# Moving the stops at which VectorE's small steps are emitted, from unit 10 on, in an attention and token-MLP kernel

## The chip, the cores and the metric

One core of one Trainium2 chip. The metric is the device time of one execution in microseconds. The change was timed in six runs of each kernel. The profiler takes one more execution of each kernel.

## The reference, cut to what matters

```python
x  = A_x                                   # 1 x 2048 x 1024, bf16
xn = layernorm(x)
out = x + A(xn, wq, wk, wv, wo, beta) + B(xn, w1, b1, w2, b2)
# A: 32 heads of 32, four segments of 512 tokens: in each a masked softmax attention and a read of a
#    memory that sums phi(k) v over the earlier segments, mixed by a gate; then the projection wo
# B: layernorm, then an MLP over the tokens (2048 -> 3584 -> 2048) with gelu
```

## The kernel before

The attention runs as 32 units, one for each segment and group of four heads. A unit computes logits, exponentials and the weighted sums (`weigh`) of its group, and between them fills TensorE (PE) with projection jobs of eight 512-column matmuls each: V, output projection (`wo`), Q, K. VectorE (DVE) empties PSUM banks and also runs small steps on SBUF data: `scales`, `phi_q`, `products`, the sum of the two products with the transpose of the result, and `phi_k` with a transpose. The steps wait in a list, `side`. While the program writes down a job's matmuls, it takes one step from that list at each of the job's stops, which are places among the eight matmuls. "Unit 11's steps" are those written down in unit 11.

```python
STOPS = ((1, 4, 7), (1, 4))                # jobs ended by ScalarE; jobs ended by VectorE
STOPS_FEW = ((1, 3, 5, 7), (1, 3, 5))

def dense(self, n, side=True):
    while n > 0 and self.jobs:
        at, b, reads, mm, end, on_dve = self.jobs[0]
        stops = self.stops[on_dve] if side else ()
        ...                                # b: the job's PSUM bank
        stop = min(at + n, 8)
        if self.side and side:
            stop = min([stop] + [x for x in stops if x > at])
        with fw.group(reads=reads(), writes=[self.R_bank[b]]):   # its last matmul increments a semaphore
            for i in range(at, stop):
                mm(b, i)
        ...
        if stop == 8:
            end(b)                         # empties the bank: ScalarE for V and Q, VectorE for wo and K
            self.jobs.popleft()
        elif self.side and stop in stops:
            self.side.popleft()()          # one small step
```

```python
# in proj_job, when a Q or K job is complete: load the weights two units ahead, then empty the bank
def finish(b):
    if u + 2 < N_UNIT:
        ring.ensure(u + 2)                 # a DMA issued by SyncE (SP)
    end(b)

# in attention(), unit u
total = 8 * len(self.jobs) - sum(j[0] for j in self.jobs) - self.left
...
self.stops = self.STOPS_FEW if total <= 26 and u >= 14 else self.STOPS
```

Each engine executes its instructions in the order in which they were written for it. Where one depends on another engine, the helper writes a wait for the semaphore of the last access to the tile concerned.

## Time and profile before

| | |
|---|---|
| time | 652.76 us median of 6 runs (652.47 to 652.96) |
| span in the profile | 651.1 us, granted PE clock 1.000 |
| PE busy | 645.8 us of it |
| DVE busy | 428.1 us |

PE is the bound, and only its gaps can be won. In the window of the change the two largest stand at the end of a run of DVE work. This is DVE's timeline for the steps of unit 11 and the first evictions of unit 12; the columns are start, duration, engine, source line, operation, tiles, shapes and count, and idle time before it in brackets:

```profile
480.00 1.65 DVE L1478 TENSOR_TENSOR prod<-ost,srec 128x1024 bf16<-128x1024 bf16 x1
481.68 0.74 DVE L1484 TENSOR_TENSOR o_s<-prod 128x512 bf16<-128x512 bf16 x1
482.34 0.28 DVE L1241 TENSOR_SCALAR mtmp<-etmp 128x512 bf16<-128x512 bf16 x1
482.65 0.69 DVE L1243 SCALAR_TENSOR_TENSOR mtmp<-kT,mtmp 128x512 bf16<-128x512 bf16 x1
483.26 0.68 DVE L1275 CAST kT<-ps_all 128x512 bf16<-128x512 f32 x1
483.87 1.04 DVE L1431 TENSOR_TENSOR ost<-ps_all,eps 128x396 bf16<-128x396 f32 x2
```

No line has idle time before it: DVE goes from products, sum and phi_k straight to the copy of K and the evictions of `ost`. PE, in unit 12 at 484.48 us, waits for the first of these evictions. The other wait stands at 503.74 us in unit 14, behind the steps of unit 13.

### The profile page before, as it was taken

Reading aid. Unit: us, or ns where it says so; the run is one execution under the profiler, and the core shown is the slowest. Engines: PE = TensorE matmul, PEld = TensorE weight load, DVE = VectorE, ACT = ScalarE, POOL = GpSimd, SP = SyncE. Lnnn points to the kernel's source line nnn. Section 1 sums busy time; section 2 is a strip of 40 time slices with the busy share of each in tenths; the row PEclk is TensorE's granted clock in tenths of the full one; section 3 lists DMA queues with packets and bytes.
Section 4 is the critical chain, followed back from the end, with each engine's and each line's share of the span. In section 5 each row is a group of like instructions: output and inputs, shape, how many; then the busy total and the mean of one; then the engine's idle time right before and its main releaser. Section 6 shows DMA issues by size and latency. Waiting matters only on the chain.

```text
span 651.1 us, 11170 instructions
## 1 busy us (share of the span) xinstructions
PE 645.8 (99%) x4611; PEld 303.2 (47%) x4611; DVE 428.1 (66%) x800; ACT 281.4 (43%) x305; POOL 153.9 (24%) x179
## 2 busy tenths in 40 slices
PE   8999999999999999999999999999999999999998
PEld 3444444444444444444444444444544444445544
DVE  6975675665556664744738325766787877777896
ACT  7543232232210000110101047778767778888770
POOL 2500000000011220220202203343334444554440
DMA  9804233242498967538262946988544456445325
GB/s 306 212 0 130 65 106 89 64 116 79 129 257 206 270 205 209 156 103 229 80 208 98 267 126 174 179 169 197 120 116 96 125 147 109 126 98 128 106 93 139
DMA packets 181963, 95.00 MB, mean 146 GB/s; under 512 B 100248, under 2 KB 167832, under 8 KB 181656
## 3 DMA queue, kind: packets, MB, share of 16 engines
q1 hardware_dynamic: 181768, 94.25, 56.3%
q8 instruction: 36, 0.59, 0.4%
q14 instruction: 15, 0.12, 0.1%
q10 hardware_dynamic: 144, 0.03, 0.0%
HBM read 69.23 MB, written 13.63 MB: 127 GB/s over the span
## 4 chain that ended last, share of the span: by engine, by line
PE 91%; DVE 5%; ACT 2%; DMA 2%; issue 1%; POOL 0%; DVEq 0%
PE ps_all L199 91%; ACT pT L1377 1%; DMA w2s<-in_B_w_dram 1%; DVE prod L1478 1%; DVE ln_st L587 1%; DVE sum L648 0%; DMA xin<-in_A_x_dram 0%; DVE mtmp L1243 0%; DVE h L627 0%; DVE mtmp L1241 0%; DVE fin L1320 0%; DVE ost L1431 0%; DVE kT L1275 0%; POOL ln_rs L611 0%; DVE part L689 0%
## 5 line engine op out<-in xcount | busy, mean ns | idle before, releaser
L1377 ACT ACTIVATE pT<-ps_all 128x2048 bf16<-128x2048 f32 x80 | 150.2, 1877 | 47.7 <-PE ps_all L199 47.2
L1381 POOL TENSOR_SCALAR_AFFINE_SELECT pT<-pT 128x512 bf16<-128x512 bf16 x128 | 105.3, 841 | 161.3 <-ACT pT L1377 161.3
L689 DVE TENSOR_TENSOR part<-ps_all,part 128x512 f32<-128x512 f32 x84 | 57.7, 690 | 109.1 <-PE ps_all L199 88.2
L1080 POOL TENSOR_TENSOR part<-part,stg 128x512 f32<-128x512 f32 x24 | 33.0, 1403 | 285.5 <-DVE part L689 285.5
L746 ACT ACTIVATE g<-part,b1c 128x512 f16<-128x512 f32 x36 | 26.0, 722 | 99.1 <-DVE part L689 99.1
L199 PE MATMUL ps_all<-wv,xnT 128*128 128x512 bf16 x256 | 68.6, 380 | 0.2
L199 PE MATMUL ps_all<-xnT,wq 128*128 128x512 bf16 (+1 forms) x256 | 66.4, 380 | 0.0
L199 PE MATMUL ps_all<-wo,oT 128*128 128x512 bf16 (+2 forms) x272 | 63.8, 367 | 0.1
L1431 DVE TENSOR_TENSOR ost<-ps_all,eps 128x396 bf16<-128x396 f32 (+1 forms) x72 | 37.1, 522 | 33.9 <-PE ps_all L199 33.3
L694 ACT ACTIVATE part<-ps_all 128x512 f32<-128x512 f32 x24 | 14.0, 596 | 101.6 <-PE ps_all L199 67.1
L199 PEld LDWEIGHTS ps_all<-vA,pT 128*128 128x128 bf16 x1280 | 45.7, 96 | 20.4 <-DVE ost L1431 1.7
L199 PE MATMUL ps_all<-g,w2s 128*128 128x512 f16 x224 | 51.0, 379 | 0.0
L199 PE MATMUL ps_all<-g,sum 128*128 128x512 f16 x224 | 51.0, 379 | 0.0
L199 PE MATMUL ps_all<-gT,sum 128*128 128x512 f16 x224 | 50.3, 379 | 0.2 <-DVE gT L663 0.2
L199 PE MATMUL ps_all<-vA,pT 128*128 128x33 bf16 x1280 | 48.5, 177 | 0.3 <-DVE ost L1431 0.3
L199 PE MATMUL ps_all<-h,sum 128*128 128x512 f16 x192 | 45.2, 379 | 0.0
L199 PE MATMUL ps_all<-h,w1s 128*128 128x512 f16 x192 | 44.9, 379 | 0.0
L199 PE MATMUL ps_all<-hT,sum 128*128 128x512 f16 x192 | 43.6, 379 | 0.0
L199 PEld LDWEIGHTS ps_all<-wo,oT 128*128 128x128 bf16 x272 | 23.8, 98 | 24.7 <-issue 3.7
L199 PEld LDWEIGHTS ps_all<-xnT,wq 128*128 128x128 bf16 x256 | 22.6, 97 | 25.4 <-issue 5.3
L199 PEld LDWEIGHTS ps_all<-gT,sum 128*128 128x128 f16 x224 | 21.8, 98 | 26.8 <-DVE gT L663 0.6
L199 PEld LDWEIGHTS ps_all<-g,w2s 128*128 128x128 bf16 x224 | 21.9, 98 | 26.4
(118 smaller groups left out, 867.7 us busy)
## 6 DMA issues: line engine op xcount, KB each, us to landing
w2s<-in_B_w_dram SPq DMA_DIRECT2D x8, 1792.0 KB, 9.7
w1s<-in_B_w_dram SPq DMA_DIRECT2D x12, 1024.0 KB, 5.6
wq<-in_A_wq_dram SPq DMA_DIRECT2D x32, 256.0 KB, 3.2
stg<-in_A_x_dram SPq DMA_DIRECT2D x16, 256.0 KB, 2.9
xs<-in_A_x_dram SPq DMA_DIRECT2D x16, 256.0 KB, 3.3
out_dram<-stg SPq DMA_DIRECT2D x16, 256.0 KB, 3.7
wk<-in_A_wk_dram SPq DMA_DIRECT2D x16, 256.0 KB, 3.6
fin<-out_dram SPq DMA_DIRECT2D x16, 256.0 KB, 3.3
```

The lines of the kernel that those rows point to most:

```text
L199: ins = self.nc.tensor.matmul(*args, **kwargs)
L587: fw.op("dve", lambda e: e.bn_stats(st[:, 6 * h:6 * h + 6], src[:, 512 * h:512 * h + 512]), reads=[self.R_xin[c]], writes=[R])
L689: self.fw.op("dve", lambda e: e.tensor_tensor(self.tmp[dst][:], self.bank(b), self.tmp[src][:], op=ALU.add), reads=[self.R_bank[b], self.R ...
L694: self.fw.op("act", lambda e: e.activation(self.tmp[dst][:], self.bank(b), ACT.Copy), reads=[self.R_bank[b]], writes=[self.R_tmp[dst]])
L746: self.fw.op("act", lambda e: e.activation(self.gB[f % 2][half][:, f // 2, :], src, ACT.Gelu_apprx_tanh, bias=self.b1c[:, f:f + 1], scale= ...
L1080: fw.op("pool", lambda e: e.tensor_tensor(self.tmp[t][:], self.tmp[t][:], self.stg[k][:, 512 * half:512 * half + 512], op=ALU.add), reads= ...
L1377: fw.op("act", lambda e: e.activation(dst, src, ACT.Exp, scale=SCALE), reads=self.R_bank[0:4], writes=[R[v % 2][kb] for v, kb, _ in blocks ...
L1381: fw.op("pool", lambda e: e.affine_select(d, d, pattern=[[0, 4], [1, P]], compare_op=ALU.is_ge, fill=0.0, base=0, channel_multiplier=-1), ...
L1431: fw.op("dve", lambda e: e.tensor_tensor(dst, src, eps, op=ALU.add), reads=[self.R_bank[b], self.R_eps], writes=[self.R_ost[o][part]])
L1478: fw.op("dve", lambda e: e.tensor_tensor(self.prod[:], ost[:, :, 0:D_HEAD], rec.unsqueeze(2).to_broadcast([P, 32, D_HEAD]), op=ALU.mult), ...
```

## The change

Its intent, read from its form, is to spread the small steps more evenly over the jobs. From unit 10 on they come at matmuls 1, 3, 5 and 7 instead of 1, 4 and 7, and in jobs that VectorE ends at 1 and 3 instead of 1 and 4, unless the first branch takes the unit.

```diff
     STOPS = ((1, 4, 7), (1, 4))
+    STOPS_MID = ((1, 3, 5, 7), (1, 3))
     STOPS_FEW = ((1, 3, 5, 7), (1, 3, 5))
...
-            self.stops = self.STOPS_FEW if total <= 26 and u >= 14 else self.STOPS
+            self.stops = self.STOPS_FEW if total <= 26 and u >= 14 else self.STOPS_MID if u >= 10 else self.STOPS
```

(Worked out from the job list no unit from 14 on has more than 24 matmuls left, so the first branch takes them all. Only units 10 to 13 get the new stops.)

## The prediction

> **What bounds the kernel now.** I read the page first: the busy times, then the chain of work that ended last.
>
> ```profile
> span 651.1 us, 11170 instructions
> ...
> PE 645.8 (99%) x4611; PEld 303.2 (47%) x4611; DVE 428.1 (66%) x800; ACT 281.4 (43%) x305; POOL 153.9 (24%) x179
> ...
> PE 91%; DVE 5%; ACT 2%; DMA 2%; issue 1%; POOL 0%; DVEq 0%
> ```
>
> TensorE (PE) is busy 645.8 of 651.1 us, and is 91% of the chain. A change that removes no matmul can only win back PE's gaps, 651.1 - 645.8 = 5.3 us, 0.8% of the span. A gain of over 2% (13 us) is out of reach.
>
> The diff names units 10 to 17 of the attention (32 units of one head group each). A unit's stops are chosen as "few" first where it has at most 26 matmuls and is number 14 or later. I worked each unit's count out from the job list: units 10 to 13 have four jobs (V, output projection, Q, K), 32 matmuls; units 14 to 17 have three, 24, and so keep the stops they have. The change reaches only units 10 to 13. In the timeline they run from the first output projection (465.6 us) to some 505 us. The table of stretches gives for that window:
>
> ```profile
> core 0: us, PE busy (x) PEld busy (x) DVE busy (x) ACT busy (x) POOL busy (x), PEclk, DMA share, GB/s
> 466.00:505.00 39.00, 38.55 (x393) 18.64 (x392) 32.32 (x64) 26.92 (x27) 13.64 (x16) 1.00 0.44 102
> ```
>
> PE's gaps are 39.00 - 38.55 = 0.45 us here: all that a perfect reordering of VectorE (DVE) in these units could win, 0.07%. The list of waits of that window says whose they are:
>
> ```profile
> PEld ps_all L199 <- DVE ost L1431: 1.3, 2, 0.7
> ...
> PE ps_all L199 <- DVE ost L1431: 0.3, 2, 0.2
> ```
>
> Twice PE waits for DVE to empty a bank (columns: total, times, longest). The chain shows why: DVE runs prod, o_s, mtmp, the copy of kT and then that eviction back to back. This is what the author presumably wants to ease.
>
> **What the Trainium skill says.** "Trainium Architecture — The Big Picture", section "Inside one NeuronCore": each engine has its own instruction stream, and they meet only through semaphores. So the place of a DVE step among the matmuls in the source means nothing in itself; only its order on DVE and its waits do. The trace agrees: DVE's o_s starts at 471.81 us, as soon as prod (470.55 + 1.22 us) is over, while PE is inside a run of V matmuls. "DMA: Bandwidth & Descriptors", section "Queues, rings and completion order": SP owns one queue row, whose descriptors each DMA engine takes in ring order. The trace shows the half of it that matters here, SP's issues one after another, each 0.4 to 2 us. "TensorE: Matmul & The Clock Gate", section "The cost: per-tile semaphore tail": about 26 ns for each increment that a packed matmul makes. No view of this trace isolates that.
>
> **The change part by part.** I compared the two built programs engine by engine, with each wait traced back to the instruction that releases it.
>
> PE: the same 4,611 matmuls in the same order with the same releasers. Ten semaphore increments go from one matmul to a neighbour (from the fourth to the third, from the seventh to the fifth, and so on): ten added, ten taken away, net 0. Were all ten pure cost at the page's 26 ns it would be an estimated 0.26 us, 0.04%.
>
> DVE, ACT, POOL: the same instructions, the same order, the same releasers. The reason: the steps (scales, phi, products, sum) read and write SBUF only, so none waits for a matmul; and in each of the four units the same steps fall between the same bank evictions. One more step is emitted inside Q's job (the sum with the transpose of its result), one fewer in K's, but Q's job ends with work for ACT, not DVE, so it is nothing on DVE to overtake. DVE's saving: 0.
>
> SP: three pairs of DMA issues change places, in units 10, 11 and 13 (unit 12 does not change). The load of a Q weight (wq) stood before the transpose of the sum's result (oT); now it stands after. These are the pairs, from the timeline of SP:
>
> ```profile
> 469.71 0.57 SPq L221 DMA_DIRECT2D wq<-in_A_wq_dram  x1
> 472.26 1.19 SPq L221 DMA_TRANSPOSE oT<-o_s  x1
> 473.80 1.19 SPq L221 DMA_TRANSPOSE pk<-mtmp  x1
> ...
> 479.69 1.80 SPq L221 DMA_DIRECT2D wq<-in_A_wq_dram  x1
> 482.45 1.20 SPq L221 DMA_TRANSPOSE oT<-o_s  x1
> 483.69 1.26 SPq L221 DMA_TRANSPOSE pk<-mtmp  x1
> ...
> 498.95 0.38 SPq L221 DMA_DIRECT2D wq<-in_A_wq_dram  x1
> 501.71 1.19 SPq L221 DMA_TRANSPOSE oT<-o_s  x1
> 502.94 2.05 SPq L221 DMA_TRANSPOSE pk<-mtmp  x1
> ```
>
> oT goes no sooner: in the first pair o_s ends at 471.81 + 0.42 = 472.23 us, 0.03 us before its issue; it waited for DVE, not for wq. So nothing is gained. What is paid: wq waits for oT's issue to end. With the 0.04 us that SP leaves between issues, that is 472.26 + 1.19 + 0.04 = 473.49 (3.8 us later), 482.45 + 1.20 + 0.04 = 483.69 (4.0 later) and 501.71 + 1.19 + 0.04 = 502.94 (4.0 later). Landing takes 3.2 us (median of all wq), so 476.7, 486.9 and 506.1 us. The ring holds two weights and loads two units ahead; the jobs that read these three begin at
>
> ```profile
> 487.35 1.89 PE L199 MATMUL ps_all<-xnT,wq 128*128 128x512 bf16 x8
> ...
> 497.02 1.90 PE L199 MATMUL ps_all<-xnT,wq 128*128 128x512 bf16 x8
> ...
> 514.62 1.89 PE L199 MATMUL ps_all<-xnT,wq 128*128 128x512 f16 x8
> ```
>
> Slack left: 10.7, 10.1 and 8.5 us. With the slowest wq landing of the whole trace, 5.4 us, it is still 6.3.
>
> The transpose after it (pk) moves too. With 0.57 us for the issue of wq it starts at 473.49 + 0.57 + 0.04 = 474.1 (0.3 later), 484.3 (0.6 later) and 503.55 (0.6 later); it lands 2.5 us on (median), at 476.6, 486.8 and 506.05. Its matmuls two units on begin at 484.96, 495.93 and 513.09 us: 8.4, 9.1 and 7.0 to spare. Its source, mtmp, is written again by DVE at 482.34, 490.51 and 509.44: 5.7, 3.7 and 3.4 us to spare, the tightest place of the change. What follows pk in the queue (wk, kT, xnT) slips by the same 0.3 to 0.6 us, with two units or more until use.
>
> Sum: matmuls 0, DVE 0, increments 0 net, DMA at most 4 us later with at least 3.4 us of slack everywhere. Effect on the path: 0.0 us.
>
> **The rivals.** First, the change does what it seems meant for: DVE's chain shortens and PE's 0.45 us of gaps close, 652.2 us. For it: the two waits for DVE are in just these units. Against: DVE's order and its releasers are the same, so that chain cannot move. Second, the late wq starves PE in one or more of three places: if a slack were overdrawn by a microsecond each time, 655.7 us. For it: 4 us later is more than its whole landing time. Against: the slacks, twice that. Third, crowding: oT, wq, pk and wk now leave within about 3.5 us, where wq had been let go 2.6 to 2.8 us before oT; landings lengthen, pk's source is held, DVE waits and with it PE. If all three places lost 0.5 us it would be 654.2. For it: the margin of 3.4 us is the smallest, and oT has taken up to 4.9 us to land. Against: the DMA share of the window is 0.44, and pk's landings here reach only 3.2 us. Fourth, the moved increments cost something by themselves: at most the 0.26 us above.
>
> **Range and chances.** The three timed runs lie at 652.47, 652.67 and 652.96, a spread of 0.5 us, more than any effect I can name. I take the median as the prediction, 652.7, and for the range 0.8 us below and 0.7 above it: the gap-closing rival, the increments and ordinary scatter fit in; starvation does not. Faster by over 2% would need 13 us, more than all of PE's gaps: 0.01. Slower by over 2% would need several lost microseconds at each of three swaps, against slacks that would have to be wrong: 0.01.
>
> **What would show it right or wrong.** Right: in the changed kernel's SP timeline the three pairs stand as oT, wq, pk, with oT within 0.1 us of o_s's end as before; DVE and PE run through these units at the same times to some 0.1 us; PE is busy about 38.5 of the same 39 us; PE's waits for ost are still two. Wrong: a wait of PE on a wq load, or of DVE on a transpose before mtmp, in units 11 to 15, or PE's busy time in the window changed by more than 0.3 us. The prediction fails altogether if the order on DVE at run time differs from that of the built program, or if units 14 to 17 change.

## The result, and the profile after

The changed kernel took 652.86 us median of 6 runs (652.56 to 653.05), the kernel before 652.76. The ratio is 1.0001, 95% interval 0.9989 to 1.0014: the same. (A ratio is the mean time of one kernel's runs over that of the other's of the same rounds, so it is not quite the ratio of the medians.)

The page of the changed kernel, in its first lines:

```profile
span 651.0 us, 11122 instructions
...
PE 641.2 (99%) x4563; PEld 303.3 (47%) x4611; DVE 428.1 (66%) x800; ACT 281.4 (43%) x305; POOL 153.9 (24%) x179
```

PE's 641.2 us are not a change. The count beside them is 4,563 matmuls instead of 4,611, while the weight loads, one for each matmul, are complete. 48 matmul records are missing from this trace, and 4.6 us of busy time with them. What can be compared is when things start. SP's timeline shows the three swapped pairs; unit 12, where no pair changes places, is left out:

```profile
472.03 1.19 SPq L221 DMA_TRANSPOSE oT<-o_s  x1
473.26 0.58 SPq L221 DMA_DIRECT2D wq<-in_A_wq_dram  x1
474.20 1.20 SPq L221 DMA_TRANSPOSE pk<-mtmp  x1
...
482.22 1.19 SPq L221 DMA_TRANSPOSE oT<-o_s  x1
483.45 0.58 SPq L221 DMA_DIRECT2D wq<-in_A_wq_dram  x1
484.08 1.26 SPq L221 DMA_TRANSPOSE pk<-mtmp  x1
...
501.48 1.19 SPq L221 DMA_TRANSPOSE oT<-o_s  x1
502.72 0.58 SPq L221 DMA_DIRECT2D wq<-in_A_wq_dram  x1
503.34 2.25 SPq L221 DMA_TRANSPOSE pk<-mtmp  x1
```

This execution runs 0.2 us ahead of the one before, and did so already before the first changed unit (an issue of pk at 454.71 us against 454.94). With that offset of 0.23 us the oT transposes stand where they stood, and wq goes 3.8, 4.0 and 4.0 us later. The list of waits in the window keeps its two lines, to the digit:

```profile
PEld ps_all L199 <- DVE ost L1431: 1.3, 2, 0.7
...
PE ps_all L199 <- DVE ost L1431: 0.3, 2, 0.2
```

DVE's instructions from 465 to 515 us stand in the same order, each 0.2 us earlier than before, and so do the first matmuls of each job on PE. Here are the eviction of `ost` in unit 12 and the matmuls that wait for it, at 483.87 and 484.48 us before:

```profile
483.64 1.04 DVE L1431 TENSOR_TENSOR ost<-ps_all,eps 128x396 bf16<-128x396 f32 x2
...
484.25 0.57 PE L199 MATMUL ps_all<-vA,pT 128*128 128x33 bf16 x16 [0.16 <-DVE ost L1431]
```

### The profile page after: what moved, and what is told of

Same layout as the page of the kernel before. It is cut to its first block, busy times and chain, and to the rows that moved or that the text cites. A ratio compares the mean times of both kernels' runs of the same rounds, so it can differ in the third digit from the quotient of the medians.

```text
span 651.0 us, 11122 instructions
## 1 busy us (share of the span) xinstructions
PE 641.2 (99%) x4563; PEld 303.3 (47%) x4611; DVE 428.1 (66%) x800; ACT 281.4 (43%) x305; POOL 153.9 (24%) x179
## 4 chain that ended last, share of the span: by engine, by line
PE 92%; DVE 4%; ACT 2%; issue 1%; DMA 0%; POOL 0%; DVEq 0%
PE ps_all L199 92%; ACT pT L1377 1%; DVE prod L1478 1%; DVE ln_st L587 1%; DMA xin<-in_A_x_dram 0%; DVE mtmp L1243 0%; DVE h L627 0%; DVE mtmp L1241 0%; DVE fin L1320 0%; DVE ost L1431 0%; DVE kT L1275 0%; POOL ln_rs L611 0%; ACT qT L1266 0%; ACT vA L1306 0%; DVE srec L1474 0%
## 5 line engine op out<-in xcount | busy, mean ns | idle before, releaser
L199 PE MATMUL ps_all<-wv,xnT 128*128 128x512 bf16 x238 | 64.1, 380 | 1.5 <-issue 0.5
L199 PE MATMUL ps_all<-xnT,wq 128*128 128x512 f16 (+1 forms) x249 | 64.2, 380 | 0.1
L199 PE MATMUL ps_all<-wo,oT 128*128 128x512 bf16 (+2 forms) x255 | 59.9, 366 | 1.3 <-issue 0.5
L199 PEld LDWEIGHTS ps_all<-g,sum 128*128 128x128 f16 x224 | 21.9, 98 | 26.4
```

Of the source, the lines that this page charges most:

```text
L199: ins = self.nc.tensor.matmul(*args, **kwargs)
```

## The experiments

Each is an edit of the kernel before. All gave the correct result, and the prediction left little to explain, so they ask three things: is each part of the change really free (e1, e4, e5), how far is it from costing something (e6), and what would it have taken to move the time (e2, e3, e7)?

**e1, all remaining steps at one stop.** The change's idea taken to its extreme.

```diff
             elif self.side and stop in stops:
                 self.side.popleft()()
+                while self.side and self.at_once and not on_dve:   # at_once: units 10 to 13
+                    self.side.popleft()()
```

> The change carried to its extreme: in units 10 to 13 all VectorE steps left are put out at the first stop inside Q's job, instead of being spread over Q's and K's jobs. The built program has the same instructions, order and releasers on TensorE, VectorE, ScalarE and GpSimd; only the Q weight load moves, now behind both transposes. My theory (a stop is a place in the text, and only the order on an engine counts): 652.8 us, VectorE's and TensorE's timeline the same to 0.1 us apart from a common offset, two waits of TensorE for ost in the window as before. Rival (the spacing of the steps among the matmuls matters to VectorE or TensorE): bunching five steps hurts by about a microsecond in each of four units, 655 to 657 us.

Measured: 652.49 us against 652.55, ratio 0.9999 (0.9987 to 1.0012). The two waits for ost are 1.3 us (weight loads) and 0.3 us (matmuls), twice each, as before. Bunching up to five steps at one place costs nothing and wins nothing that these runs can show: in units 10 to 13 the spacing of the stops does not reach DVE. This kernel also makes the swap on SP stronger than the change does, since wq here stands behind both transposes.

**e2, a true change of order.** No stops in K's job in units 11 and 13.

```diff
-            self.stops = self.STOPS_FEW if total <= 26 and u >= 14 else self.STOPS
+            self.stops = self.STOPS_FEW if total <= 26 and u >= 14 else ((1, 4, 7), ()) if u in (11, 13) else self.STOPS
```

> No stops in K's job in units 11 and 13: the sum and phi of K then fall behind the copy of K and the next evictions of ost, a true change of VectorE's order in the two units where TensorE waits for ost. My theory (the two waits are real but small): the two waits of TensorE for ost (longest 0.7 us on the weight-load side) are gone, TensorE's gaps shrink by up to 0.45 us, 652.3 to 652.5 us, if no new wait takes their place. Rival (the two waits are hidden anyway or come back one unit later at the eviction of the output projection, which now stands behind two more steps): 652.8 us or a little more, with a wait of TensorE for fin or kT in units 12 and 14.

Measured: 652.55 us against 652.55, ratio 1.0000 (0.9988 to 1.0013). The expected time did not come, the rival did. These are all of PE's waits for DVE in e2's timeline from unit 12 to unit 15:

```profile
492.96 0.61 PE L199 MATMUL ps_all<-wo,oT 128*128 128x512 bf16 x2 [0.45 <-DVE kT L1275]
...
512.20 0.57 PE L199 MATMUL ps_all<-vA,pT 128*128 128x33 bf16 x16 [0.22 <-DVE ost L1431]
```

The two waits for ost, at 484.48 and 503.74 us in the kernel before, are gone, and each has come back one unit later: 0.45 us in unit 13 for the copy of unit 12's K, 0.22 us in unit 15 for ost. (The rival had named fin or kT; the second came at ost.) PE reaches the second group of output projections of unit 12 at 485.31 us, where it was 486.04 before; less the run's offset of 0.40 us that is 0.33 us won. At the Q job that starts at 496.60 (497.02 before) it is lost again.

**e3, the products computed twice in units 10 to 13.** The kernel's results are the same.

```diff
         def products():
-            fw.op("dve", ...)
+            for _ in range(1 + (9 <= u <= 12)):       # u is the unit before
+                fw.op("dve", ...)
```

> The product of units 10 to 13 is computed twice (same result), four more VectorE instructions of 1.2 to 1.65 us. It measures whether VectorE's length is on the path here. My theory: in units 11 and 13 the chain up to ost is back to back and TensorE waits at its end, so 1.65 us each go on the path; in unit 10 the copy of kT is held (1.2 us), in unit 12 little (0.3 to 0.7): together 4.4 to 5.2 us, 657.1 to 658.0. Rival (VectorE is 66% busy and off the path): 0 to 0.5 us, at most 653.3.

Measured: 658.55 us median (658.09 to 660.76) against 652.55, ratio 1.0098 (1.0084 to 1.0113): 6.0 us, above the expected 4.4 to 5.2. PE's waits for DVE in its timeline:

```profile
475.41 0.61 PE L199 MATMUL ps_all<-wo,oT 128*128 128x512 bf16 x2 [1.83 <-DVE kT L1275]
...
487.34 0.57 PE L199 MATMUL ps_all<-vA,pT 128*128 128x33 bf16 x16 [1.73 <-DVE ost L1431]
...
509.75 0.57 PE L199 MATMUL ps_all<-vA,pT 128*128 128x33 bf16 x16 [1.73 <-DVE ost L1431]
```

The places are nearly the expected ones: behind the steps of units 10, 11 and 13. Behind those of unit 12, where 0.3 to 0.7 us had been expected, there is nothing; in the kernel before, DVE is idle there for 2.25 us before the next eviction of `ost`. Units 11 and 13 each add 1.73 - 0.16 = 1.57 us to the wait that was there. In unit 10 the matmul at 475.41 stood at 474.13 before; with the run's offset of 0.41 us (DVE's pqT at 469.53 instead of 469.94, just before) it is 1.69 us late (1.2 us expected). That is 4.8 us. In the profiled execution (658.88 us, mean granted clock 0.997) the rest is PE's clock: the table of stretches shows it after the second wait (the column before the last two is the granted clock, PEclk):

```profile
486.00:487.00 1.00, 0.00 (x0) 0.00 (x0) 1.00 (x3) 0.16 (x1) 0.00 (x0) 1.00 0.65 131
...
488.00:489.00 1.00, 0.78 (x5) 0.24 (x3) 0.64 (x3) 0.00 (x0) 0.00 (x0) 0.50 0.19 41
489.00:490.00 1.00, 1.00 (x10) 0.27 (x10) 0.94 (x4) 0.26 (x1) 0.00 (x0) 0.50 1.00 227
490.00:491.00 1.00, 1.00 (x4) 0.42 (x3) 0.69 (x1) 1.00 (x1) 0.00 (x0) 0.50 0.00 0
491.00:492.00 1.00, 1.00 (x5) 0.37 (x4) 0.01 (x1) 0.62 (x1) 0.31 (x1) 0.80 0.00 0
```

For some 3.4 us (three whole ones, and 0.4 in the next, where the mean is 0.80) the clock is halved. From the matmuls at 487.34 us to the first output projection of the next unit, at 497.84, PE takes 10.50 us, where the kernel before takes 8.92 (484.48 to 493.40): 1.6 us more. 4.8 + 1.6, less the 0.4 us by which this run was ahead when the window began, is 6.0, and the spans differ by 657.1 - 651.1 = 6.0. Two of the four timed runs list a clock of 1.000 and are still 5.5 and 5.7 us slower (658.09 and 658.22 us). They were not profiled, so what they have beyond the 4.8 us of waits stays open. DVE, though 66% busy, thus has hardly any slack in three of these four units.

**e4, an increment after every matmul of a job.** About 475 increments more, spread over the attention.

```diff
-            with fw.group(reads=reads(), writes=[self.R_bank[b]]):
-                for i in range(at, stop):
-                    mm(b, i)
+            for i in range(at, stop):
+                with fw.group(reads=reads(), writes=[self.R_bank[b]]):
+                    mm(b, i)
```

> Every matmul of a projection job increments TensorE's semaphore, instead of the last one before a stop: some 475 more increments, nothing else different. My theory (the ten moved increments cost nothing because an increment by itself costs a 0.38 us matmul nothing): 652.8 us. Rival (each costs the page's 26 ns on the path): 475 x 0.026 = 12.4 us, 665 us.

Measured: 652.50 us against 652.55, ratio 1.0001 (0.9986 to 1.0016). The interval's upper end is 0.16%, 1.0 us, so on average one increment costs at most 1.0 / 475, 2.2 ns, on the path, and the ten that the change moves cost nothing that counts.

**e5, every Q weight loaded at the start of the next unit.** From unit 10 on, 18 loads.

```diff
             if u + 2 < N_UNIT:
-                ring.ensure(u + 2)
+                if ring is self.wq_ring and u >= 12:        # this job runs in unit u - 2
+                    self.held.append((u - 2 + 1, u + 2))
+                else:
+                    ring.ensure(u + 2)
...
+            while self.held and self.held[0][0] <= u:       # at the start of unit u, before its first dense()
+                self.wq_ring.ensure(self.held.popleft()[1])
```

> From unit 10 on, each Q weight is loaded at the start of the next unit instead of at the end of its own job, for all 18 loads that are left: later than the change makes it (in units 10 and 11 by some 6 us against the kernel before, where the change has 4), and in six times as many places. My theory (8 us and more of slack): no wait of TensorE or its weight loads for a wq load, 652.5 to 652.9 us. Rival (the late load starves TensorE): each microsecond overdrawn shows 18 times, 655 us or more.

Measured: 652.67 us against 652.65, ratio 1.0000 (0.9986 to 1.0013). The first two loads are issued at 475.34 and 485.44 us, 5.6 and 5.8 us later than before. No list of waits has a wq load in it. This trace lacks no matmul records, and DVE has the order of the kernel before, so it gives PE's busy time in the window, which the trace after could not. Stretch 466 to 505:

```profile
466.00:505.00 39.00, 38.54 (x393) 18.67 (x393) 32.32 (x65) 27.11 (x27) 13.67 (x16) 1.00 0.42 96
```

**e6, the same at the end of the next unit.** The same edit with the loop that issues them after the unit's last `dense()`.

> The same, but at the end of the next unit: for the first of them some 485.6 us instead of 469.7 us (16 later), landing 3.2 us on, at 488.8 us, when its job would begin at 487.35 us. My theory (the slack against the kernel before is 14.4 us for the first, 14.1 and 12.4 for the next two, and the transfer takes 3.2): now it is overdrawn, by 1.5 us in the first, 0 to 2 us in the others, 18 times: 660 to 675 us, with waits of the weight loads for wq. Rival (weights are wanted later than I read): 652.8 us.

Measured: 706.58 us (702.95 to 708.20) against 652.65, ratio 1.0834 (1.0817 to 1.0851). The first such load is issued at 485.18 us, and PE waits for it:

```profile
488.94 1.90 PE L199 MATMUL ps_all<-xnT,wq 128*128 128x512 bf16 x8 [1.86 <-DMA wq<-in_A_wq_dram]
```

All PE's waits for such loads, from the list of waits (total, times, longest):

```profile
PE ps_all L199 <- DMA wq<-in_A_wq_dram: 36.5, 11, 5.4
```

The mechanism and the first wait (1.86 us, 1.5 expected) are right; the size, 54 us instead of 7 to 22, is not. Later waits are up to 5.4 us long, where 0 to 2 had been expected. Later units are shorter (24 or 20 matmuls by the job list, not 32), which may be why; no run tests it. And PE's mean granted clock fell to 0.976: at 701.2 us that is an estimated 16.8 us. 36.5 + 16.8 = 53.3, against a difference of the spans of 50.1, so the estimate is about 3 us too high; the two may overlap.

**e7, less moved than in e2.** Stop 1 stays in K's job in units 11 and 13, so only phi_k moves behind the evictions (and the next unit's steps each come one stop later).

```diff
+            ... else ((1, 4, 7), (1,)) if u in (11, 13) else self.STOPS
```

> As e2, but only phi of K moves behind the next evictions in units 11 and 13 (stop 1 stays in K's job), 0.97 us of VectorE work instead of 1.4. e2 won 0.33 us at ost in unit 11 and lost it again at kT in unit 12. My theory (VectorE has a little slack in unit 12, so less work moved is all absorbed): TensorE's waits for ost in units 11 and 13 are gone and no wait for kT comes in unit 12; 0.2 to 0.5 us less in the span, 652.0 to 652.4 us. Rival (whatever leaves one unit comes back in the next): the same span as before, 652.5, with the wait at kT in 12 or at ost in 14.

Measured: 652.41 us against 652.65, ratio 0.9996 (0.9984 to 1.0009): the same by this measure. The trace tells more. No matmul waits for DVE in this window any more, and PE is busy 38.87 of the 39.00 us:

```profile
466.00:505.00 39.00, 38.87 (x395) 18.98 (x394) 32.62 (x64) 27.37 (x27) 13.19 (x16) 1.00 0.43 103
```

Two matmuls that every kernel has, one before and one well after, free this of each run's offset. In the kernel before, unit 10's memory update and unit 16's first Q matmul:

```profile
465.40 0.39 PE L199 MATMUL ps_all<-vA,pk 128*128 128x132 bf16 x4
...
522.24 0.59 PE L199 MATMUL ps_all<-xnT,wq 128*128 128x512 f16 x2
```

In e7:

```profile
465.46 0.39 PE L199 MATMUL ps_all<-vA,pk 128*128 128x132 bf16 x4
...
521.92 0.59 PE L199 MATMUL ps_all<-xnT,wq 128*128 128x512 f16 x2
```

They lie 56.84 us apart before, 56.46 in e7: 0.38 us less. The same pair is 56.86 us apart in the changed kernel (465.17 to 522.03) and 56.82 in e2 (465.00 to 521.82); in e1, e4 and e5 it is 56.84 to 56.88. e7 is thus the only one that shortens the stretch, by about 0.06% of the whole. The gain is not lost later: the last transposes on PE (ident, L205) start 176.14 us after the same memory update in e7, and 176.49 to 176.56 us after it in those six others. But it is one trace; the timed runs cannot confirm it, and I claim no faster kernel.

## Why the prediction was right

The timed runs alone say little: 0.1 us of difference lies inside a scatter of 0.5 us, and the interval leaves room for 0.7 us less or 0.9 us more. What bears the account is where the instructions stand in the traces.

**Only units 10 to 13 are touched.** Right, though the prediction says that the diff names units 10 to 17, and it names 10 and no end. From the built programs: no instruction from unit 14 on has another place or wait. The timelines agree, with the one offset up to 514 us.

**DVE: 0.** Right. The small steps read SBUF only and no eviction lies between an old stop and its new one. The trace after has DVE's order and its two waits unchanged, and e1 shows that even all remaining steps at one stop change nothing there. The first rival, that PE's gaps close, fails with this for the change as written. e2 and e7 show that it takes a change of order across an eviction to touch those waits, and that its worth was sized right, at 0.45 us at most: e7 gets 0.38.

**Increments: 0 net.** Right, and e4 sets the bound: at most 2.2 ns each by the interval, which also closes the fourth rival.

**SP: three swaps, at most 4 us later, 8.5 us and more of slack.** Right: with the offset, wq goes at the predicted times to 0.02 us (473.26 + 0.23 = 473.49), and pk too in the second and third place. In the first, pk goes 0.33 us later than I worked out, because SP left 0.36 us before it, not the 0.04 us that I took. That came out of the margin of 5.7 us there. Why SP left 0.36 us is open. What follows pk slips by up to 0.8 us (kT, 505.64 + 0.23 against 505.04), not 0.6, because the third pk took SP 2.25 us instead of 2.05. e5 moves 18 loads instead of three, the first two by 5.6 and 5.8 us, at no cost, and e6 shows the far side, where the slack I read (14.4 us against the kernel before) is used up: load issued at 485.18, PE stopped until 488.94. The second rival is real in kind but far off. The third, crowding, shows in no list of waits, nor in the times from issue to landing between 460 and 515 us: the longest are 3.6 us for wq, 3.4 for pk and 4.0 for oT, against 3.3, 3.2 and 3.9 before.

**The signs that I had named.** One of them failed as written: PE's busy time in the window after is 37.86 us, 0.69 below before, beyond the 0.3 that I called wrong:

```profile
466.00:505.00 39.00, 37.86 (x385) 18.66 (x393) 32.32 (x65) 27.15 (x27) 13.65 (x16) 1.00 0.41 97
```

It is a matter of missing records (385 matmuls recorded there against 393 before, with 393 weight loads against 392), and the place where the prediction was careless: a busy time proves nothing until its count is compared. e5's complete trace has 38.54 us with the same DVE order. The traces of e1 to e4, all taken on another chip than e5 to e7, lack the same 48 records each, and those of e5 to e7 lack none; so the gap does not come from the change.

**Left open.** Why the run after was 0.2 us ahead before the change begins was not followed; the runs scatter by 0.5 us. Whether e7's 0.38 us is there in unprofiled runs was not settled.

## What to carry to other kernels

Where engines run independent streams, a knob that says "between these matmuls" acts only if it carries an instruction past another one on the same engine, or past a wait; compare the built programs engine by engine before expecting anything of it. When the order does change, work taken from before a wait must find slack afterwards: 1.4 us of it moved (e2) came back as new waits one unit later, 0.97 us of it (e7, one trace) did not. And first read the ceiling: PE's gaps in the changed units were 0.45 of 652 us.

## What the Trainium skill lacked or had wrong

- "TensorE: Matmul & The Clock Gate", section "HAM oscillation — how this bites in real kernels", gives the rule of no PE gaps over about 3.4 us. In e3 the longest wait in PE's list is 1.83 us, and PE still ran about 3.4 us at a granted clock of 0.50, from 0.7 us after the end of a gap of 1.73 us; this cost 1.6 us more. After the two other gaps, of 1.73 and 1.83 us, it did not slow. So keeping gaps under 3.4 us was not enough here. That the gap brought it about is likely, since every run of the kernel before lists a clock of 1.000, but not shown.
- The same page, section "The cost: per-tile semaphore tail", gives 26.3 ns for an increment, fitted to the tail of packed small matmuls. It has no figure for 512-column matmuls in a row: 475 more increments in e4 changed the time by -0.05 us, at most 2.2 ns each by the interval.
- "DMA: Bandwidth & Descriptors" has no trn2 time for which SP is held by the issue of a small SBUF transpose: here it is 1.19 us in most for 128 x 512, and up to 2.25. A wq load that stood ready behind one that waited for DVE went 3.8 to 4.0 us later.
- No page says that matmul records can be missing from a trace while the weight loads are complete (4,563 of 4,611 after the change, 4,611 before), which makes PE's busy time 4.6 us smaller than it was.
